# Putting the first loads of an MLP kernel on one DMA queue instead of two

## The chip, the cores and the metric

The kernel runs on one core of a Trainium2 chip. The metric is the device time of one execution in microseconds (us). TensorE is called PE below; SyncE (SP) and ScalarE (ACT) are the two engines whose sequencers issue DMA transfers here, each on a queue of its own.

## The reference

```python
# x (1, 2048, 576), w1 (576, 4608), b1 (4608), w2 (4608, 576), b2 (576), all bf16
h = einsum("bsd,df->bsf", x, w1) + b1
r = where(h > 0, h, 0)
out = einsum("bsf,fd->bsd", r * r, w2) + b2
```

## The kernel before

The 2048 rows are worked in four blocks of 512. For block 0, x comes as four tiles of 128 rows, is transposed on PE and copied to `xTw`. The first 512 columns of w1 (`w1n`) are multiplied first. Four row pieces of 128 (k = 0 to 3) use the whole array. The last 64 rows (`w1n8`) make the "pair products", two half arrays side by side. The rest of w1 (`w_h`) follows, also as pairs. While PE waits for the first data it runs warm-up products on constants.

```python
WARM = [512] * 6 + [256]                       # columns of the warm-up products
...
load_x(nc.sync, 0)
load_x(nc.scalar, 1)
load_x(nc.sync, 2)
load_x(nc.scalar, 3)
for k in range(NK):                            # NK = 4
    load_w1n(nc.sync if k % 2 == 0 else nc.scalar, k, k + 1)
...
keep(nc.scalar.dma_start(out=b1_rows[0:NFT, :], ...))
for h in range(2):
    load_w1n8(nc.sync, h)
...
# block 0, in PE's program order
for j in range(2):        x_transpose(j)       # five 128x128 transposes each
x_copies(0)                                    # VectorE and ScalarE: PSUM to xTw, rows 0-255
for j in range(2, RT):    x_transpose(j)
x_copies(1)
dup_windows(0)
for k in range(NK):       part(0, k)           # 4 products of 256 rows each
part(1, 0)
make_b1T()
for k in range(1, NK):    part(1, k)
# ... the pair products with w1n8, then w_h
```

Of the kernel before, what the change touches and what calls it, by code (L numbers as in the profile page):

```python
# [17 lines left out]
def kernel(  # L18
# [9 lines left out]
    nc = tc.nc  # L28
# [9 lines left out]
    NK = NC // 2  # L38
# [6 lines left out]
    RT = SB // P  # L45
# [12 lines left out]

    wps = ps_h.tile([P, 512], FP32, name="wps", tag="ph")
    ones = nc.const_aps.tensor(1.0, [P, 512], BF16)  # L60
    WARM = [512] * 6 + [256]
    for i, n in enumerate(WARM):
        keep(nc.tensor.matmul(wps[:, 0:n], lhsT=ones[:, 0:P], rhs=ones[:, 0:n], start=True, stop=True))  # L63

# [6 lines left out]
    def load_x(eng, rt):  # L71
        keep(eng.dma_start(out=xs[:, rt, :], in_=x2[rt * P:(rt + 1) * P, :]))  # L72

    def load_w1n(eng, k0, k1):
        src = w1[k0 * P:k1 * P, 0:GW].rearrange("(k p) f -> p k f", p=P)
        keep(eng.dma_start(out=w1n[:, k0:k1, :], in_=src))
# [7 lines left out]

    b1_rows = const.tile([P, P], BF16, name="b1_rows")
    nc.vector.memset(b1_rows[:], 0.0)
    load_x(nc.sync, 0)
    load_x(nc.scalar, 1)
    load_x(nc.sync, 2)
    load_x(nc.scalar, 3)  # L90
    for k in range(NK):
        load_w1n(nc.sync if k % 2 == 0 else nc.scalar, k, k + 1)

    ident = const.tile([P, P], BF16, name="ident")
    make_identity(nc, ident[:])
# [28 lines left out]

    w2_sb = wpool.tile([P, NFT, D], BF16, name="w2_sb")
    w2_view = w2.rearrange("(ft p) d -> p ft d", p=P)
    W2CH = 18

    def load_w2(c):
        keep(nc.sync.dma_start(out=w2_sb[:, c * W2CH:(c + 1) * W2CH, :], in_=w2_view[:, c * W2CH:(c + 1) * W2CH, :]))  # L130

# [154 lines left out]
    b2T = const.tile([P, 1], FP32, name="b2T")  # L286
    nc.gpsimd.tensor_copy(out=b2T[:], in_=b2_col[:])
    keep(nc.sync.dma_start(out=b2_bc[:], in_=b2.partition_broadcast(P)))
    for c in range(2):
        load_w2(c)  # L290
    load_xT(2)

# [51 lines left out]
```

## Time and profile before

Three runs took 290.65, 290.67 and 291.33 us; the profiled one took 290.52. These are the lines that matter from the page of the profiled run: the span, PE's busy time with its share and number of instructions, and by engine the chain of work that ended last.

```profile
span 288.7 us, 4690 instructions
...
PE 284.6 (99%) x2027; PEld 138.9 (48%) x2032; DVE 78.6 (27%) x177; ACT 96.5 (33%) x152; POOL 0.9 (0%) x7
...
PE 97%; DMA 1%; SPq 0%; issue 0%; DVE 0%
```

PE is busy for 99% of the span and has 97% of the chain. The loads can matter only at the start, before PE has work without a wait. The chain in order of time (start, length, what) and then the timeline of PE (start, length, engine, line, operation, operands, count) show that start.

```profile
0.73 0.40 SPq L72
...
1.20 0.44 SPq L72
1.68 3.68 DMA w1n<-in_w_dram
5.41 2.36 PE pn L217 x20
```

```profile
3.76 1.52 PE L146 MATMUL tb<-ident,x_sb 128*128 128x128 bf16 x20
5.41 2.36 PE L217 MATMUL pn<-xTw,w1n 128*128 128x256 bf16 x20
7.60 0.22 PE L159 MATMUL b1T_ps<-ident,b_rows 128*128 128x128 bf16 x1
7.66 1.47 PE L217 MATMUL pn<-xTw,w1n 128*128 128x256 bf16 x12
9.06 0.39 PE L196 MATMUL pn<-xTw,w1n 64*128 64x512 bf16 x1
```

The w1n transfer that was issued at 1.68 us (k = 0) landed 3.68 us later, at 5.36, and PE's first w1n product started at 5.41. From there 20 and 12 products and the small transpose run without a break up to the pair products at 9.06 us.

Two more views are needed. The first is the table of stretches; its columns are: stretch, its length and PE's busy time (instructions), then busy time of PEld, DVE, ACT and POOL, the granted clock, the DMA engines' mean busy share, and what they moved in GB/s. The second is that of the x tiles: nanoseconds least, median and most, and microseconds from issue to landing.

```profile
1.75:5.75 4.00, 3.77 (x30) 1.89 (x28) 1.22 (x6) 1.90 (x3) 0.00 (x0) 1.00 0.98 300
```

```profile
L146 PE MATMUL tb<-ident,x_sb x20: 219/219/230, 3.8 to 5.1; 128*128 128x128 bf16 x20
...
DMA to landing us min/median/max: 2.8/3.0/3.2
```

A transpose of 219 ns is one at full clock; at half clock it takes longer. (The clock column of the stretches doesn't tell the two apart at the start, since nothing is recorded before the first full-clock record. The trace's own clock records begin at 3.66 us here.)

### The profile page before, as it was taken

The numbers are of one execution on the slowest core, as the hardware profiler recorded it, in microseconds if no ns is written. First come the engines' busy times: TensorE is split into PE (matmuls) and PEld (weight loads), VectorE is DVE, ScalarE is ACT, GpSimd is POOL, SyncE is SP. The second block draws the span as 40 slices with busy tenths as digits, with TensorE's granted clock in tenths as the row PEclk, the third lists the DMA queues.
The fourth block names the chain that finished last, engine by engine and source line by source line (L and its number), as shares of the span: only waits on it lengthen the run. The fifth ranks groups of instructions, "written<-read, shape, count | busy, mean of one in ns | idle before, by whom it ended". The sixth has DMA issues, their size and how long they took to land.

```text
span 288.7 us, 4690 instructions
## 1 busy us (share of the span) xinstructions
PE 284.6 (99%) x2027; PEld 138.9 (48%) x2032; DVE 78.6 (27%) x177; ACT 96.5 (33%) x152; POOL 0.9 (0%) x7
## 2 busy tenths in 40 slices
PE   8999999999999999999999999999999999999996
PEld 5544444444444555555544444444444455555555
DVE  3444544444500200000025444444440001100001
ACT  3666666666500000000027666666670000000000
POOL 0000000000000000000000000000000000000000
PEclk9999999999999999999999999999999999999999
DMA  6999999600001100000000000000000110000000
GB/s 198 236 244 197 265 388 246 94 0 2 0 18 36 37 16 18 16 16 18 16 16 2 1 2 0 2 0 2 0 2 0 36 39 16 16 16 19 32 17 18
DMA packets 31573, 16.59 MB, mean 57 GB/s; under 512 B 15552, under 2 KB 31552, under 8 KB 31552
## 3 DMA queue, kind: packets, MB, share of 16 engines
q1 hardware_dynamic: 30928, 15.72, 22.3%
q10 hardware_dynamic: 624, 0.57, 0.7%
q8 instruction: 16, 0.26, 0.4%
q14 instruction: 5, 0.04, 0.0%
HBM read 11.43 MB, written 2.36 MB: 48 GB/s over the span
## 4 chain that ended last, share of the span: by engine, by line
PE 97%; DMA 1%; SPq 0%; issue 0%; DVE 0%
PE ph L181 42%; PE po L272 38%; PE pt L253 11%; PE pn L202 4%; DMA w1n<-in_w_dram 1%; PE pn L217 1%; PE ph L183 1%; PE pn L196 1%; SPq L72 0%; DVE o_sb L274 0%; PE b1T_ps L159 0%; PE pn L198 0%
## 5 line engine op out<-in xcount | busy, mean ns | idle before, releaser
L181 PE MATMUL ph<-xTw,w_h 64*128 64x512 bf16 x576 | 124.6, 376 | 0.0
L183 PE MATMUL ph<-xTw,w_h 64*128 64x512 bf16 x576 | 124.6, 376 | 0.0
L272 PE MATMUL po<-w_sb,hT 128*128 128x448 bf16 (+2 forms) x612 | 109.4, 341 | 0.0
L169 ACT ACTIVATE r<-ph,b1T 128x512 bf16<-128x512 f32 x128 | 81.1, 685 | 41.6 <-PE ph L183 41.6
L181 PEld LDWEIGHTS <-w_h 64*128 64x128 bf16 x576 | 54.1, 94 | 68.3
L272 PEld LDWEIGHTS <-hT 128*128 128x128 bf16 x612 | 58.5, 98 | 51.0
L170 DVE TENSOR_TENSOR hT<-r 128x512 bf16<-128x512 bf16 x144 | 61.2, 426 | 76.9 <-ACT r L169 76.9
L183 PEld LDWEIGHTS <-w_h 64*128 64x128 bf16 x576 | 54.1, 94 | 0.0
L274 DVE TENSOR_TENSOR o_sb<-po,b_bc 128x448 bf16<-128x448 f32 (+2 forms) x17 | 10.2, 597 | 125.8 <-PE po L272 125.8
L253 PE MATMUL pt<-hT,w_sb 128*128 128x512 bf16 x142 | 31.3, 379 | 0.1
L169 ACT ACTIVATE r<-pn,b1T 128x512 bf16<-128x512 f32 x16 | 10.3, 688 | 62.0 <-PE pn L198 60.6
L253 PEld LDWEIGHTS <-w_sb 128*128 128x128 bf16 x144 | 14.1, 98 | 17.0
L256 ACT ACTIVATE oT<-pt,b2T 128x512 bf16<-128x512 f32 x4 | 2.7, 687 | 28.3 <-PE pt L253 28.3
L202 PE MATMUL pn<-xTw,w1n 128*128 128x512 bf16 x45 | 10.4, 379 | 0.4 <-issue 0.3
L202 PEld LDWEIGHTS <-w1n 128*128 128x128 bf16 x48 | 4.5, 98 | 6.0 <-issue 0.8
L217 PE MATMUL pn<-xTw,w1n 128*128 128x256 bf16 x32 | 3.7, 273 | 0.1
L63 PE MATMUL wps<-const-bfloat16-1.0 128*128 128x512 bf16 (+1 forms) x7 | 2.9, 597 | 0.8 <-PEq L328 0.8
L217 PEld LDWEIGHTS <-w1n 128*128 128x128 bf16 x32 | 3.0, 98 | 0.6 <-DMA w1n<-in_w_dram 0.3
L115 DVE COPY xTw<-xTw 64x2048 bf16<-64x2048 bf16 x4 | 2.8, 690 | 0.6 <-ACT xTw L152 0.5
L116 DVE COPY xTw<-xTw 64x2048 bf16<-64x2048 bf16 x4 | 2.8, 688 | 0.1
L196 PE MATMUL pn<-xTw,w1n 64*128 64x512 bf16 x8 | 2.4, 379 | 0.0
L198 PE MATMUL pn<-xTw,w1n 64*128 64x512 bf16 x8 | 2.4, 379 | 0.0
(21 smaller groups left out, 10.5 us busy)
## 6 DMA issues: line engine op xcount, KB each, us to landing
w_sb<-in_w_dram SPq DMA_DIRECT2D x2, 2592.0 KB, 15.2
w_h<-in_w_dram SPq DMA_DIRECT2D x14, 288.0 KB, 6.6
out_dram<-o_sb SPq DMA_DIRECT2D x15, 112.0 KB, 1.7
w_h<-in_w_dram SPq DMA_DIRECT2D x4, 144.0 KB, 3.2
out_dram<-ot SPq DMA_DIRECT2D x4, 128.0 KB, 2.0
x_sb<-in_x_dram ACTq DMA_DIRECT2D x2, 144.0 KB, 3.0
x_sb<-in_x_dram SPq DMA_DIRECT2D x2, 144.0 KB, 3.0
w1n<-in_w_dram ACTq DMA_DIRECT2D x2, 128.0 KB, 3.6
```

The lines of the kernel that those rows point to most:

```text
L63: keep(nc.tensor.matmul(wps[:, 0:n], lhsT=ones[:, 0:P], rhs=ones[:, 0:n], start=True, stop=True))
L115: keep(nc.vector.tensor_copy(out=xT[0:H, SPC:SPC + 4, :], in_=xT[H:P, E3:E3 + 4, :]))
L169: keep(nc.scalar.activation(out=r[:], in_=bank[:], func=ACT.Relu, bias=b1T[:, ft:ft + 1], scale=1.0))
L170: keep(nc.vector.tensor_tensor(out=hTs[sb][:, ft, :], in0=r[:], in1=r[:], op=ALU.mult))
L181: keep(nc.tensor.matmul(bx[:], lhsT=w1_h[0:H, LO_C[i], jc], rhs=xT[0:H, LO_W[i], :], start=(i == 0), stop=(i == NC - 1)))
L183: keep(nc.tensor.matmul(by[:], lhsT=w1_h[H:P, UP_C[i], jc], rhs=xT[H:P, UP_W[i], :], start=(i == 0), stop=(i == NC - 1)))
L196: keep(nc.tensor.matmul(banks[2 * i][:], lhsT=w1n8[0:H, 2 * i * P:(2 * i + 1) * P], rhs=xT[0:H, SPC, :], start=start, stop=stop, skip_grou ...
L202: keep(nc.tensor.matmul(banks[g][:], lhsT=w1n[:, k, g * P:(g + 1) * P], rhs=xT[:, O + k, :], start=start, stop=stop))
L217: keep(nc.tensor.matmul(banks[g][:, hc], lhsT=w1n[:, k, g * P:(g + 1) * P], rhs=xT[:, O + k, hc], start=(h == 0 and k == 0), stop=False, s ...
L253: keep(nc.tensor.matmul(pt[:], lhsT=w2_sb[:, ft, DM:D], rhs=hT[:, ft, :], start=(i == 0), stop=(i == NFT - 1)))
L272: keep(nc.tensor.matmul(po[:, 0:d1 - d0], lhsT=hT[:, ft, jj * P:(jj + 1) * P], rhs=w2_sb[:, ft, d0:d1], start=(i == 0), stop=(i == NFT - 1)))
L274: keep(nc.vector.tensor_tensor(out=o_sb[:, d0:d1], in0=po[:, 0:d1 - d0], in1=b2_bc[:, d0:d1], op=ALU.add))
```

## The change

All four x tiles and the first w1 group are issued by SyncE alone, w1n in three transfers instead of four (k = 2 and 3 together); ScalarE issues only the first bias. The warm-up is shortened by 384 columns, and W2, wanted much later, comes in three transfers instead of two. The intent is an earlier x tile 0, and a ScalarE that is free early.

```diff
-    WARM = [512] * 6 + [256]
+    WARM = [512] * 5 + [384]
@@
-    load_x(nc.sync, 0)
-    load_x(nc.scalar, 1)
-    load_x(nc.sync, 2)
-    load_x(nc.scalar, 3)
-    for k in range(NK):
-        load_w1n(nc.sync if k % 2 == 0 else nc.scalar, k, k + 1)
+    for rt in range(RT):
+        load_x(nc.sync, rt)
+    for k0, k1 in [(0, 1), (1, 2), (2, NK)]:
+        load_w1n(nc.sync, k0, k1)
@@
-    W2CH = 18
+    W2CH = 12
@@
-    for c in range(2):
+    for c in range(3):
         load_w2(c)
```

## The prediction

> **What bounds the kernel now.** TensorE. The page has PE busy 284.6 of 288.7 us; the chain of waits gives PE 97%. Only the start can move: in the chain, issue and the w1n transfer lead until 5.36 us; from 5.41 us on PE waits for nothing the change touches. The timeline of the first 10 us: seven warm-up matmuls 0.78 to 3.5 us at a 427 ns step (the clock is granted in full from 3.66 us); transposes of x tiles 0 and 1 start at 3.76 us on a landing, those of tiles 2 and 3 at 4.56 us on another; the first w1n matmul starts at 5.41 us on its landing; w_h matmuls start at 9.50 us.
>
> **What the change does.** ScalarE loses four issues of 0.45 us; nothing waited for its later work. SyncE goes from four such issues to seven at a step of about 0.475 us, and loses the 0.9 us it waited for an x landing before the w1n8 loads (the DMA queue's waits). Estimate from these steps: the seven end near 4.0 us, w1n8 near 5.3; the first w_h issue moves from 4.79 to about 5.3 us, 0.5 later. The Trainium skill ("DMA: Bandwidth & Descriptors", section "Issuing engines are not separate DMA queues") says a second issuing engine saves only sequencer time; the trace agrees: both queues together moved some 300 GB/s from 2 to 4 us, 0.5 us per 147 KB tile, about one issue step.
>
> What it gains: x tile 0 no longer shares the DMA engines with tile 1. Issue at 0.73, first packets 1.8 to 1.9, 0.45 us of data: landing near 3.0 instead of 3.7 us. Tiles 1, 2, 3 then follow near 3.4, 3.8, 4.3, and w1n k=0 near 4.7 to 5.0. The warm-up, shortened by 384 columns (0.32 us), frees PE at 3.2. First w1n matmul about 4.8 to 5.1 instead of 5.41: gain 0.3 to 0.6.
>
> What it loses: w1n k=2,3 are one transfer, issued last, landing near 6.0; PE would want it 0.87 us after its first w1n matmul, so waits some 0.1 to 0.4. About 0.3 remains. Then w_h: the first pair landed at 7.63 and 8.83 us and was wanted at 9.50; 0.5 later and 0.3 earlier leave about nothing. The pair for j=2,3 landed at 12.98, wanted at 13.39: it now becomes a wait of 0.1 to 0.4. So the gain is mostly given back by 13.4 us; later w_h pairs had over 1 us of slack, W2 more.
>
> **Predicted:** 290.6 us, range 289.9 to 291.5. Faster by over 2% 0.005, within 2% 0.985, slower 0.01.
>
> **What would show it.** Right: x tile 0 transposes start at 3.2 to 3.3; first w1n matmul 4.8 to 5.1; a short wait of PE for w1n near k=2; first w_h issue 5.2 to 5.4; w_h waits of PE of 0.1 to 0.4 us in 9 to 14 us; from 14 us on PE is shifted by under 0.4 us. Wrong: x tile 0 landing at 3.7; no w_h wait, so that 0.3 us or more stays; a w_h wait over 0.5 us.
>
> **What could make it wrong.** The clock. The Trainium skill ("TensorE: Matmul & The Clock Gate", section "Part 1: The HAM clock gate") says the full clock comes after about 3.4 us of activity in a free-running window; here it came 2.9 us after PE began. If the shorter warm-up missed that grant, up to 3.4 us of matmuls would run at half rate, an estimated 1.7 us lost.

## The result, and the profile after

The changed kernel took 291.44 us (median of 6 runs, 291.30 to 291.75) where the kernel before took 290.95 in the same rounds (median of 6, 290.65 to 291.33). The ratio of the two is 1.0019, with a 95% interval of 1.0006 to 1.0032. (Ratios here are the mean time of one kernel's fast runs over that of the other's of the same rounds, so not quite the ratio of the medians.) In a second job the ratio was 1.0025 (1.0011 to 1.0039): 291.56 against 290.90 us. Within 2% the two are the same; at this finer scale the change is a small loss of some 0.6 us, not a wash.

These are the same views of the changed kernel: from the page its span and PE's busy time, from the chain the lines up to the pair products (a line of issue is 0.04 us of it), from the timeline PE with the waits that end in a landing (in brackets), the stretch, and the x tiles.

```profile
span 289.6 us, 4692 instructions
...
PE 285.5 (99%) x2031; PEld 139.4 (48%) x2031; DVE 78.5 (27%) x177; ACT 96.5 (33%) x152; POOL 0.9 (0%) x7
```

```profile
3.07 0.43 SPq L76
3.50 0.04 issue
3.54 3.54 DMA w1n<-in_w_dram
7.08 0.05 issue
7.13 1.48 PE pn L215 x12
```

```profile
3.18 2.04 PE L144 MATMUL tb<-ident,x_sb 128*128 128x128 bf16 x20
5.39 0.61 PE L215 MATMUL pn<-xTw,w1n 128*128 128x256 bf16 x4 [0.16 <-DMA w1n<-in_w_dram]
6.27 0.61 PE L215 MATMUL pn<-xTw,w1n 128*128 128x256 bf16 x4 [0.27 <-DMA w1n<-in_w_dram]
7.13 1.48 PE L215 MATMUL pn<-xTw,w1n 128*128 128x256 bf16 x12 [0.25 <-DMA w1n<-in_w_dram]
...
9.91 0.39 PE L194 MATMUL pn<-xTw,w1n 64*128 64x512 bf16 x1
```

```profile
1.75:5.75 4.00, 3.84 (x29) 2.56 (x26) 1.29 (x6) 1.54 (x4) 0.00 (x0) 1.00 0.90 251
```

```profile
L144 PE MATMUL tb<-ident,x_sb x20: 219/311/312, 3.2 to 5.0; 128*128 128x128 bf16 x20
...
DMA to landing us min/median/max: 2.2/2.3/2.5
```

The x tiles do come sooner: tile 0 landed at 2.91 us instead of 3.72 and its transposes began at 3.18. But the first w1n product starts at 5.39, as before, because w1n k = 0 landed at 5.34. Then PE waits again for k = 1 (6.22) and again for the merged k = 2, 3 (7.08). The three landings are 0.87 us apart although the issues are 0.47 us apart. The chain now goes through the last of them, and the pair products start at 9.91 us instead of 9.06.

From the pair products on nothing differs. The span less the start of the pair products is 279.69 us before (288.75 less 9.06) and 279.67 after (289.58 less 9.91), and 279.68 to 279.69 in the repeats below. The whole loss lies before that point. The profile shows it as 0.85 us, more than the 0.6 us of the timed rounds; the repeats explain that.

### The profile page after: what moved, and what is told of

Read it like the earlier page. It is cut to its first block, busy times and chain, and to the rows that moved or that the text cites. A ratio compares the mean times of both kernels' runs of the same rounds, so it can differ in the third digit from the quotient of the medians.

```text
span 289.6 us, 4692 instructions
## 1 busy us (share of the span) xinstructions
PE 285.5 (99%) x2031; PEld 139.4 (48%) x2031; DVE 78.5 (27%) x177; ACT 96.5 (33%) x152; POOL 0.9 (0%) x7
## 4 chain that ended last, share of the span: by engine, by line
PE 97%; DMA 1%; SPq 1%; issue 0%; DVE 0%
PE ph L179 42%; PE po L270 38%; PE pt L251 11%; PE pn L200 4%; DMA w1n<-in_w_dram 1%; PE pn L215 1%; PE ph L181 1%; PE pn L194 1%; SPq L72 1%; SPq L76 0%; DVE o_sb L272 0%; PE b1T_ps L157 0%; PE pn L196 0%
```

## The experiments

The facts of every profile in one table. "k=2" is the landing of the w1n transfer that holds k = 2; "last" is the last landing of the four w1n pieces; "pairs" is the start of the first pair product; "clock" is the first full-clock record of the trace ("none": that trace holds no clock record). Landings and clock are read from the trace's semaphore and clock records. GB/s is that of 1.75 to 5.75 us in the view of stretches.

| Run | x and w1n transfers (SP+ACT) | GB/s | k=2 | last | pairs | clock | ratio to before (95%) |
|---|---|---|---|---|---|---|---|
| before | 4+4 | 300 | 6.06 | 6.06 | 9.06 | 3.66 | |
| before_r1 | 4+4 | 290 | 6.54 | 6.74 | 9.37 | 5.58 | |
| before_r2 | 4+4 | 295 | 6.51 | 6.51 | 9.34 | 3.90 | |
| b_w2c3 | 4+4 | 299 | 6.35 | 6.35 | 9.22 | 3.83 | 0.9997 (0.9983-1.0010) |
| b_inter2 | 4+4 | 292 | 6.67 | 6.84 | 9.50 | 5.55 | 1.0003 (0.9991-1.0016) |
| b_pairs | 2+2 | 318 | 5.88 | 5.88 | 9.09 | 4.03 | 1.0019 (1.0000-1.0037) |
| b_pairs_r | 2+2 | 316 | 5.94 | 5.94 | 9.54 | 5.42 | |
| b_w1n_sync | 5+2 | 291 | 6.36 | 6.36 | 9.62 | 6.33 | 0.9998 (0.9986-1.0010) |
| b_x_sync | 6+2 | 281 | 6.53 | 6.53 | 11.74 | 9.74 | 1.0021 (1.0003-1.0039) |
| after | 7+0 | 251 | 7.08 | 7.08 | 9.91 | 4.77 | 1.0019 (1.0006-1.0032) |
| after_r1 | 7+0 | 257 | 6.73 | 6.73 | 9.56 | 5.71 | 1.0025 (1.0011-1.0039) |
| after_r2 | 7+0 | 245 | 7.21 | 7.21 | 10.04 | 3.40 | |
| a_w1n4 | 8+0 | 229 | 6.92 | 7.29 | 9.75 | 4.55 | 1.0019 (1.0006-1.0031) |
| a_oldwarm | 7+0 | 236 | 7.43 | 7.43 | 10.26 | none | 1.0029 (1.0017-1.0042) |
| a_xpairs | 5+0 | 287 | 6.94 | 6.94 | 9.77 | 4.78 | 1.0006 (0.9994-1.0018) |
| a_w1n1 | 5+0 | 253 | 7.15 | 7.15 | 12.40 | 3.58 | 1.0086 (1.0049-1.0124) |
| a_x1w2 | 3+0 | 289 | 6.50 | 6.50 | 11.70 | 9.09 | 1.0097 (1.0077-1.0118) |
| a_x1w2_r | 3+0 | 278 | 7.34 | 7.34 | 12.11 | 9.58 | |

All gave the right result. Names that begin with b edit the kernel before, those with a the changed one.

My theory after the first profile: on one queue the w1n pieces land later, and PE waits for k = 2. The rivals: the shorter warm-up cost clock; the later issue times set the landings; the merging of k = 2 and 3 is to blame; or small transfers on one queue leave the DMA engines idle between them, whatever the number of queues.

### The whole w1 group in one transfer (a_w1n1)

```diff
-    for k0, k1 in [(0, 1), (1, 2), (2, NK)]:
+    for k0, k1 in [(0, NK)]:
```

> The changed kernel with the first w1n group in one transfer of 512 KB (six transfers on SyncE instead of seven). In the changed kernel the three w1n transfers landed at 5.34, 6.22 and 7.08 us, 0.87 us apart, although they were issued 0.47 us apart. Theory A (on a single queue each transfer boundary leaves the DMA engines idle for a while, which two queues hide): with two boundaries fewer the last byte lands clearly earlier than 7.08, at 6.3 to 6.7 us. Rival B (a single queue moves this data at some 150 to 200 GB/s whatever its cuts): it lands at 7.0 to 7.2. PE has to wait for the whole group in either case and then runs its 32 products without a wait: the pair products start near 10.1 (A) or 10.6 us (B) against 9.91 in the changed kernel; time 291.5 to 292.2 us.

The single transfer landed at 7.15 us: rival B's figure, not A's. So taking the cuts out of w1n did not bring the last byte sooner. (In this profile x tiles 2 and 3 also landed later, at 4.56 and 5.25 us.) The expected start of the pair products was far off under either theory: 12.40 us. By the timeline PE sat idle for 0.51 and 0.23 us before x tiles and for 1.45 us before its first w1n product at 7.20, and the trace's clock records say what that did. The full clock came at 3.58 us, fell to half at 6.99 and returned at 10.40, so all of the w1n products to that point ran at half rate. The time, 1.0086, is therefore no measure of the transfer. It is uncertain for another reason too: two of its six runs, at 296.3 and 296.6 us, had a mean clock of 0.987 to 0.988.

### x in two transfers (a_xpairs)

```diff
-    for rt in range(RT):
-        load_x(nc.sync, rt)
+    for r in (0, 2):
+        keep(nc.sync.dma_start(out=xs[:, r:r + 2, :],
+                               in_=x2[r * P:(r + 2) * P, :].rearrange("(r p) d -> p r d", p=P)))
```

> The changed kernel with x tiles 0 to 3 in two transfers of two tiles; w1n still in three on SyncE. The first w1n issue moves from 2.60 to about 1.66 us, 0.94 earlier, while the bytes ahead of it stay the same. Rival I (the SyncE issue rate sets when w1n lands): w1n lands about 0.9 earlier, at 4.4, 5.3 and 6.1 us. Theory A (DMA engines on one queue, with a bubble at each boundary): two boundaries fewer, so only some 0.2 to 0.4 us earlier, at about 5.0, 5.9 and 6.7. Time 290.9 to 291.2 us under A, 290.5 to 290.8 under I.

The first w1n issue moved from 2.60 to 1.76 us. Its landing did not come sooner at all: 5.78 us, then 6.18, and 6.94 for k = 2, 3. That refutes rival I: a transfer issued 0.8 us earlier landed no earlier. Theory A's 5.0 for k = 0 failed as well, though its 6.7 for the last piece was nearer. But the rate rose from about 250 to 287 GB/s, so the size of the transfers does play a part in the rate. The time is between the two kernels, 1.0006, and its interval includes 1 (at 291.45 us it lies above what either theory expected). The chain shows the same form as in the changed kernel:

```profile
2.73 4.20 DMA w1n<-in_w_dram
...
6.98 1.48 PE pn L216 x12
```

### Each half of the change alone (b_w1n_sync, b_x_sync)

```diff
 # b_w1n_sync: the kernel before, its w1n loop replaced by
+    for k0, k1 in [(0, 1), (1, 2), (2, NK)]:
+        load_w1n(nc.sync, k0, k1)
 # b_x_sync: the kernel before, its four x loads replaced by
+    for rt in range(RT):
+        load_x(nc.sync, rt)
```

> The kernel before with only the w1n part of the change: x on both queues as before, w1n in three transfers on SyncE, and nothing of the rest. If the single queue for w1n is the cause, w1n lands late: SyncE issues it from 1.68 to about 3.1, and I expect landings near 5.1, 5.9 and 6.6, so most of the loss (0.3 to 0.6 us of the 0.85 us by which the first w_h matmul moved in the profile). If x on one queue is the cause, no loss.

> The kernel before with only the x part of the change: the four x tiles on SyncE, w1n on both queues as before (so ScalarE issues its two w1n parts at 0.73 us, beside the first x tiles), old warm-up. Two queues stay busy, so the whole 1.1 MB should land by 6.1 to 6.4 us, but x tile 3 and w1n k=0 and 2 come last. If the single queue for w1n is the cause of the loss, this one is within 0.2 us of before; if x on one queue is the cause, it loses 0.3 us or more.

With w1n alone on SyncE, and x on both queues, the last piece landed at 6.36 us, within the range of the kernel before, and the time did not change (0.9998). The expected loss is not there. With x alone on SyncE the ratio is 1.0021, against my expectation for the theory that w1n on one queue is the whole cause. But that run also lets two w1n pieces overtake x (x tiles 2 and 3 landed at 5.41 and 5.76), so it is not a clean half. What the w1n run says is that merging k = 2 and 3 and issuing all of w1n on SyncE do no measurable harm as long as x uses the other queue as well. The x run can't say which of its two differences costs the time.

The x run shows a second thing. Its six runs fall in two groups, 291.4 to 291.7 and 293.1 to 293.2, and the profile is of the second group: it got the full clock only at 9.74 us. The profile of b_w1n_sync got it at 6.33, and its transposes show it, in the view of the x tiles:

```profile
L146 PE MATMUL tb<-ident,x_sb x20: 314/314/314, 3.5 to 5.5; 128*128 128x128 bf16 x20
```

Its pair products started at 9.62 us for that reason (its k = 2 had landed at 6.36, and PE shows no idle time before them), yet its time equals that of before. So a single profile of this start carries a clock of its own, and the kernels had to be profiled again.

### Both kernels again (before_r1, before_r2, after_r1, after_r2)

> The kernel before once more, for its spread. Theory C (the full clock comes at a moment that changes from run to run; the profile of before had it early, at 3.66 us): if it comes after 5.4 us here, the pair products start at up to 9.06 plus half of the time between 5.4 us and the grant, so at 9.2 to 9.7 us, and the span is longer by the same; if it comes by 5.4 us they start at 9.0 to 9.2. Theory L (what differs between the two kernels is when the w1n transfers land): the four w1n parts land within 0.2 us of 5.2, 5.4, 5.8 and 6.1 in every run of this kernel.

> As the run before it. Theory C: start of the pair products follows the moment of the full clock, 9.0 to 9.2 us for a grant by 5.4 us, up to 9.7 for one near 6.8. Theory L: last w1n part at 5.9 to 6.3 us.

> The changed kernel once more, timed. Theory L: its w1n parts land near 5.3, 6.2 and 7.1 us again (within 0.3), and the pair products start 2.8 us after the last of them, at 9.8 to 10.2, whatever the moment of the full clock as long as that is by 7 us. Theory C alone (the w1n landings do not matter): the pair products move with the grant as in the kernel before. Time over before: ratio 1.001 to 1.003.

> As the run before it: theory L, last w1n landing 6.8 to 7.4 us and pair products at 9.8 to 10.2; theory C alone, pair products within 9.0 to 9.7 by the grant.

The changed kernel keeps theory L's rule exactly. In its three profiles the pair products start at 9.91, 9.56 and 10.04 us, with the merged transfer landing at 7.08, 6.73 and 7.21: 2.83 us before, each time, while the clock came at 4.77, 5.71 and 3.40. The clock is not on its chain. These are the chain lines of the two new profiles:

```profile
3.56 3.18 DMA w1n<-in_w_dram
...
6.78 1.48 PE pn L215 x12
```

```profile
3.55 3.66 DMA w1n<-in_w_dram
...
7.26 1.48 PE pn L215 x12
```

For the kernel before, both expectations were partly wrong. The landings are not within 0.2 us from run to run: k = 2 came at 6.06, 6.54 and 6.51. And the grant at 3.90 us went with pair products at 9.34, later than theory C allowed. The chain went through the landing of k = 0 in two of the profiles, and through the half-clock transposes in the other, of which these are lines:

```profile
0.78 2.93 PE wps L63 x7
3.71 2.07 PE tb L146 x20
5.78 2.29 PE pn L217 x20
```

The first profile of before was thus a lucky one. The mean start of the pair products in three profiles each is 9.26 us before (9.06, 9.37, 9.34) and 9.84 after: 0.58 us. The timed rounds say 0.0019 to 0.0025 of 291 us, 0.55 to 0.73 us. The two accounts agree.

Why a later k = 2 costs so much is also to be read here. In the kernel before, PE wants k = 2 about 0.87 us after its first w1n product, so at 6.28 us in the first profile and near 6.5 in the repeats; it landed 0.2 us ahead and then just in time. In both repeats the pair products start 2.83 us after the landing of k = 2 (9.37 less 6.54, 9.34 less 6.51), as in the changed kernel; in before_r1 the first k = 2 product starts about 0.1 us late for it, a wait too short for the chain to list. That transfer had next to no slack, so nearly all of its delay reaches PE.

### k = 2 and k = 3 apart (a_w1n4)

```diff
-    for k0, k1 in [(0, 1), (1, 2), (2, NK)]:
+    for k0, k1 in [(0, 1), (1, 2), (2, 3), (3, NK)]:
```

> The changed kernel with w1n k=2 and k=3 as two transfers, so four on SyncE (eight issues). In three profiles of the changed kernel the pair products started 2.83 us after the landing of the merged k=2,3 transfer each time. Theory M (the merge holds k=2 back until k=3 has landed too): k=2 alone lands at 6.3 to 6.7 us, k=3 at 7.0 to 7.4, and the pair products start at 9.3 to 9.6 instead of 9.6 to 10.0; time some 0.3 us below the changed kernel, ratio to before 1.0003 to 1.0015. Rival B2 (each further boundary on the one queue delays all that follows by 0.2 us or so): k=3 lands at 7.3 to 7.5, pair products at 9.7 or later, ratio 1.002 or more.

Rival B2 fits better. The pieces landed at 5.30, 6.35, 6.92 and 7.29 us, the pair products started at 9.75, and the ratio is 1.0019, the same as with the merge. The merging is not the cause: PE waited for k = 1 and then found k = 2 just in time, 2.83 us ahead of the pair products as in the others. Its rate was the lowest of all, 229 GB/s with eight transfers.

### The longer warm-up, and W2 (a_oldwarm, b_w2c3)

```diff
 # a_oldwarm
-    WARM = [512] * 5 + [384]
+    WARM = [512] * 6 + [256]
 # b_w2c3
-    W2CH = 18
+    W2CH = 12
```

> The changed kernel with the longer warm-up of before. If the chain goes through the landing of w1n, the warm-up does not matter: the transposes start at 3.5 instead of 3.18 us, PE still waits for w1n, and the ratio to before is that of the changed kernel, 1.0019 to 1.0025 (within 0.0007). If instead the shorter warm-up cost something through the clock, this one is 0.2 us or more faster than the changed kernel.

> The kernel before with only the W2 part of the change (three transfers instead of two). W2 is wanted at 75 us and has landed by 48; no effect: ratio 0.9990 to 1.0010, and the pair products to the end take 279.7 us as in all profiles so far.

The old warm-up does not recover the loss: 1.0029, with an interval that overlaps those of the changed kernel. The pair products again start 2.83 us after the landing of k = 2, 3 (7.43, then 10.26). W2 in three pieces does nothing. So neither of these two edits is part of the loss.

### As few transfers as can be, on one queue and on two (a_x1w2, b_pairs)

```diff
 # a_x1w2: three transfers, all on SyncE (the loads they replace are left out here)
+    keep(nc.sync.dma_start(out=xs[:, :, :], in_=x2[0:SB, :].rearrange("(r p) d -> p r d", p=P)))
+    for k0, k1 in [(0, 2), (2, NK)]:
+        load_w1n(nc.sync, k0, k1)
 # b_pairs: two on each queue (the loads they replace are left out here)
+    for eng, r in ((nc.sync, 0), (nc.scalar, 2)):
+        keep(eng.dma_start(out=xs[:, r:r + 2, :],
+                           in_=x2[r * P:(r + 2) * P, :].rearrange("(r p) d -> p r d", p=P)))
+    load_w1n(nc.sync, 0, 2)
+    load_w1n(nc.scalar, 2, NK)
```

> The changed kernel with as few transfers on SyncE as it can have: the four x tiles in one, w1n in two (k=0,1 and k=2,3). All three are issued by 2.3 us, earlier than the last w1n issue of the kernel before (2.16 to 2.60). From 1.75 to 5.75 us the DMA engines moved 290 to 300 GB/s in the kernel before and 245 to 257 in the changed one. Theory T (many small transfers on one queue leave the engines idle between them): 285 GB/s or more here, last w1n landing 6.2 to 6.6 us. Rival Q (one queue moves less and lands later, whatever its cuts and issue times): 260 GB/s or less and last landing at 6.9 us or later. A mixed result (the rate of two queues but a late last landing, as the run with x in pairs had, 287 GB/s and 6.94 us) says that the tail of a transfer on one queue is a matter of its own.

> The same kernel once more, since landings differ by 0.3 us or so between profiles: T 6.2 to 6.6 us, Q 6.9 or later.

> The kernel before with two transfers on each of the two queues instead of four: x tiles 0,1 and w1n k=0,1 on SyncE, x tiles 2,3 and w1n k=2,3 on ScalarE. Cuts and bytes per transfer as in the run above or larger, but two queues. Q: 285 GB/s or more from 1.75 to 5.75 us and last w1n landing 6.0 to 6.6 us. T: the same. So a late landing here (6.9 or later) would speak against both, for large transfers as such landing late.

> The same kernel once more, for the spread of its landings: 6.0 to 6.6 us.

These are the stretches 1.75 to 5.75 us of a_x1w2, of its repeat, of b_pairs and of its repeat, one fence each (the last two columns are the DMA engines' busy share and GB/s):

```profile
1.75:5.75 4.00, 2.45 (x13) 1.12 (x11) 0.00 (x0) 0.47 (x2) 0.00 (x0) 1.00 0.89 289
```

```profile
1.75:5.75 4.00, 2.10 (x10) 0.77 (x8) 0.00 (x0) 0.47 (x2) 0.00 (x0) 1.00 0.86 278
```

```profile
1.75:5.75 4.00, 3.50 (x29) 1.85 (x27) 0.89 (x5) 2.27 (x4) 0.00 (x0) 1.00 0.99 318
```

```profile
1.75:5.75 4.00, 3.49 (x24) 1.99 (x22) 0.47 (x3) 1.74 (x3) 0.00 (x0) 1.00 1.01 316
```

On one queue the three large transfers moved 289 GB/s in the first profile, which is T's side, and 278 in the repeat, short of T's 285 and above Q's 260. The last landing was 6.50 us in one profile and 7.34 in the other, although the last w1n issue was at 1.79 us, earlier than in the kernel before. That is the mixed result which the expectation named. On two queues large transfers moved 316 to 318 GB/s and landed at 5.88 and 5.94 us, the earliest of all. So both matter: small transfers cost rate, on either number of queues (290 to 300 against 317 on two, 229 to 257 against 278 to 289 on one, with a_w1n1, small x and one large w1n, at 253); and one queue has the later last landing at either size.

That one queue is slower as such is shown for small transfers only. The view of stretches, asked for 1.75 to 3.75 and 3.75 to 5.75 us, gives a_x1w2 and its repeat 193 and 171 GB/s in the first half and 386 and 384 in the second; b_pairs and its repeat have 266 and 263, then 371 and 369. So three large transfers on one queue start slowly and then move as much as two queues do.

Nor do idle DMA engines explain the low rate of the small ones alone. The engines' busy share from 1.75 to 5.75 us was 0.89 to 0.92 in the three profiles of the changed kernel and 0.95 to 0.98 before, but a packet also took longer: 53 to 57 ns in the mean against 50, at nearly the same mean size (954 to 964 bytes).

Neither is a better kernel. With x tiles landing together at 4.16 us (b_pairs) or 4.89 (a_x1w2), PE idles before the transposes. In b_pairs that is 0.50 us, and the pair products start at 9.09 and 9.54 us, much as in the kernel before. Part of its loss lies elsewhere: from PE's last product to the end its span has 2.92 us where before and after have 2.66, which no run explains. In a_x1w2 PE idles for 1.55 us by the timeline, the full clock came only at 9.09 us, and the time went to 1.0097.

### An attempt at a faster start (b_inter2)

```diff
+    load_w1n(nc.sync, 0, 1)                    # after x tiles 0 and 1
+    load_w1n(nc.scalar, 1, 2)
     load_x(nc.sync, 2)
     load_x(nc.scalar, 3)
-    for k in range(NK): ...
+    load_w1n(nc.sync, 2, 3)
+    load_w1n(nc.scalar, 3, 4)
 # PE: transposes of tiles 0 and 1 interleaved; part(0, 0) and part(0, 1); transposes of 2 and 3; the rest
```

> An attempt at a faster start from what was learned: both queues as before, but the order x 0, x 1, w1n 0, w1n 1, x 2, x 3, w1n 2, w1n 3; PE transposes tiles 0 and 1 piece by piece alternately, multiplies the first half of the rows with k=0 and 1, and only then transposes tiles 2 and 3. The first w1n product should start at 4.6 to 5.0 us instead of 5.4 to 5.7, and the pair products at 8.9 to 9.2 instead of 9.06 to 9.37: ratio 0.9990 to 1.0000. If the last w1n landing (6.1 to 6.7 us) rules, as it does in the changed kernel, the pair products start 2.83 us after k=2 lands and nothing is gained.

The timeline of PE shows that the first half came true and the second did not:

```profile
4.81 1.38 PE L219 MATMUL pn<-xTw,w1n 128*128 128x256 bf16 x8
6.03 0.72 PE L148 MATMUL tb<-ident,x_sb 128*128 128x128 bf16 x10
6.72 1.48 PE L219 MATMUL pn<-xTw,w1n 128*128 128x256 bf16 x12
...
9.50 0.39 PE L198 MATMUL pn<-xTw,w1n 64*128 64x512 bf16 x1
```

The first w1n product starts 0.6 us earlier than in the first profile of before, and the pair products start at 9.50, 2.83 us after k = 2 landed (6.67). The order of the loads moved work forward, but not the landing of k = 2. The ratio is 1.0003: nothing gained. None of the runs shows a version that beats the kernel before.

## Why the prediction was right or wrong, point by point

- **Within 2%, and PE-bound after the start: right.** From the pair products on, every profile of both kernels takes 279.67 to 279.69 us.
- **x tile 0 near 3.0 us, transposes at 3.2, PE freed at 3.2: right.** Tile 0 landed at 2.91 (2.97 and 2.90 in the repeats); the transposes began at 3.18.
- **"w1n k=0 near 4.7 to 5.0", first product at "4.8 to 5.1 instead of 5.41": wrong.** It landed at 5.34, 5.38 and 5.75. The gain of 0.3 to 0.6 us never arose.
- **"w1n k=2,3 are one transfer, issued last, landing near 6.0": this is the step that failed most.** It landed at 7.08, 6.73 and 7.21. The step that failed is the rate of the loads on one queue. I took the rate that the two queues together had in the profile of before (the prediction's "the trace agrees" was no test, since that trace had both queues in use), about one 147 KB tile per issue step, and let every later landing follow the previous one at the issue step of 0.475 us. On one queue the three pieces came 0.87 us apart in the first profile, and the engines moved 245 to 257 GB/s instead of 290 to 300. A count of the packets in the traces confirms it: as many bytes as x and w1n hold (1.114 MB) had been moved by 5.42, 5.56 and 5.49 us before and by 6.12, 6.02 and 6.24 after, 0.64 us later in the mean, and k = 2 landed 0.64 us later in the mean as well (6.37 and 7.01).
- **The wait of PE for k = 2 of "0.1 to 0.4": right in kind, but not as a subtraction from a gain.** In the first profile PE waited at k = 0, at k = 1 and at k = 2, and the last landing alone sets the pair products. The sum should have been a delay of k = 2 with no slack to take it.
- **First w_h issue 5.2 to 5.4: right (5.27). A w_h wait of 0.1 to 0.4 us: wrong.** The w_h loads were issued about 0.5 us later as foreseen, but PE came later still, so nothing waited: the first pair landed at 8.44 and 8.93 us and was wanted at 10.35.
- **The clock as the danger: not the cause.** The grants in the changed kernel's profiles (4.77, 5.71, 3.40 us) do not order its pair products, and the longer warm-up did not help. The kernel before is more open to it.
- **The number.** 290.6 was meant as no change on 290.67. The kernel before itself was at 290.90 to 290.95 in the two jobs that timed the changed kernel, so 0.25 us of the miss is the small sample of the first three runs and the other 0.6 us is the mis-sized landing of w1n.

What stays open is why small transfers on one queue move fewer bytes per second, and why the last of a few large ones can still land late (in the repeat of a_x1w2 1.114 MB had been moved by 5.80 us, yet the last w1n landed at 7.34). The runs speak against the issue times, the merging and the warm-up as the cause, some of them by one profile each, and show that few large transfers restore most of the rate but not reliably the landing. One more difference was never tested alone: with ScalarE free, the 9 KB bias load is issued at 0.96 us in every one-queue run instead of 4.4 to 4.8 in the profiles of before. In b_w1n_sync and b_pairs it was issued at 1.74 and 1.88 us, and their last w1n landed no later than before (6.36 and 5.88), which makes it an unlikely cause. The trace doesn't name the DMA engine of a packet, so whether a few engines fall behind, and why, could not be followed. The landings also scatter: 6.50 to 7.43 us for the last piece in nine profiles with one queue (mean 7.07), 5.88 to 6.84 in seven with x and w1n shared evenly between two (mean 6.33). So this is a shift of the mean, not a fixed number.

## What to carry to other kernels

Before you price a change of DMA queues by its issue steps, find the one transfer with the least slack and ask when it will land; an earlier first tile is worth nothing if the last one holds the chain. Do not carry the rate that many small transfers reached on two queues over to one queue. And when the start of a kernel is at stake, profile each version several times: here a single pair of profiles showed 0.85 us where three of each and the timed rounds agree on 0.6.

## What the Trainium skill lacked or had wrong

- "DMA: Bandwidth & Descriptors", section "Issuing engines are not separate DMA queues", says that issuing from several engines only saves sequencer time. Here it did more: from 1.75 to 5.75 us four transfers on each of two queues moved 290 to 300 GB/s, seven on one queue 245 to 257. With large transfers it was 316 to 318 (two on each queue) against 278 to 289 (three on one, all issued by 2.3 us), and that gap lies wholly before 3.75 us. The last w1n landing came 0.7 us later on one queue in the mean (7.07 against 6.33 us).
- The same page, section "Rules for kernel authors", asks for large transfers for bandwidth. That agrees in the rate (317 against 290 to 300 GB/s on two queues), but the page doesn't weigh it against the wait for the first tile: with x in two transfers PE's transposes started at 4.20 us instead of 3.51 to 3.76, and the time was not better (1.0019).
- "TensorE: Matmul & The Clock Gate", "Part 1: The HAM clock gate", gives a free-running window of 3413 ns. One run agrees closely: full clock at 3.58, half at 6.99, full at 10.40 us, each 3.41 apart. The page gives no figure for the share of a window that must be busy. Here the full clock came between 3.40 and 5.71 us after the span's start in the profiles of these two kernels, with PE busy from 0.78, and as late as 9.1 to 9.7 us in three profiles whose first w1n product came late, at 6.5 to 7.4 us.
